# RetNet attention and SwiGLU FFN on one core: the first stage written as one list of steps, with other places for loads, jobs 8 to 11, norms and rounding

## The chip, the cores and the metric

The kernel runs on one core of a Trainium2 chip. The metric is the time of the program on the device in microseconds (us). The engines of a core are named as in the profile: PE (TensorE), DVE (VectorE), ACT (ScalarE), POOL (GpSimd) and SP (SyncE, which issues most DMAs here). Each engine works through its own instructions in program order, and SP's DMAs are issued in the order in which they stand in its queue.

## The reference

```python
# attention: batch 8, heads 8, seq 576, head_dim 64
scores = scale * np.matmul(q, k.transpose(0, 1, 3, 2))
Dmat = np.where(rel >= 0, gamma[:, None, None] ** rel[None, :, :], 0.0)
ret = scores * Dmat[None, :, :, :]
out = np.matmul(ret, v).astype(np.float32)
# FFN on its result: 4608 tokens, d_model 512, d_ff 1536
rms = np.sqrt(np.mean(x * x, axis=-1, keepdims=True) + 1e-06)
xn = x / rms * rms_g
g = xn @ w_gate
silu = g * (1.0 / (1.0 + np.exp(-g)))
val = xn @ w_val
return (silu * val @ w_out).astype(np.float32)
```

The decay `gamma` differs by head; the attention's result, seen as 4608 tokens of 512, is the input of the RMS norm and the FFN. Everything is float32.

## The kernel before

The attention is cut into 32 jobs, a pair of heads of one batch each; four jobs fill one unit of tokens `u` (512 tokens; there are nine). For a job, `load_first`/`load_tails` (jobs 0 to 7) or `fetch` (from job 8 on) load q, k, v; `turn` (jobs 0 to 7, on PE with ACT copying out) or `prepare` (from job 8 on, DVE's transposes, L256) bring q and k into the transposed layout; `scale_v` multiplies v by decay factors on ACT (L265); `slot(j)` issues the matmuls: the values of the job before (L354, L374), and its own scores (L284) and states (L304). `close(j)` issues the values of a job without a slot following. `fetch` issues 13 DMAs on SP: four for q and four for k (L159), two each for k and v (L200), one for v's tail (L203). They wait, if at all, for the buffers of an earlier job.

The FFN of units 2 to 8 uses a block scheme with fewer products (`up`, L594, and `across`, L735), which needs the weights rounded and combined beforehand. That happens in the first stage, `start()`. The weights come in 36 halves (`load_half`, through SP, L858). For each half DVE and ACT extract exponents (`exponent`), mantissas (`mantissa`, L891 and L895), and `join` (L912) puts them together. `weights(n)` goes on by n of these steps, and `weights_to(n)` until n halves are joined. Every fourth half completes a set: POOL combines its blocks (`combine_blocks`, L923), and SP stores them (L948): the `up` sets to `w_up_blocks`, the three `out` slices to `w_out_blocks`, seven stores each. `store_blocks` issues such stores, and `refill` loads pieces of `w_out_blocks` back into the ring of buffers (L564). `act(n)` does n waiting pieces of the jobs' ACT and DVE work (masks, sums, results).

Units 0 and 1 are computed in this stage with `up_plain`: 48 products (`up`, L655) of four 128x128x512 matmuls each, k even for gate (ACT's Silu) and odd for value (a DVE multiply). Then `across(0)` and `across(1)` multiply by w_out, after which `up(2)` begins, which reads the sums of x that `sums_of_x(2)` (L527) makes.

The norm of unit u: `square` (ACT, L430) per job; `gather` (DVE, L440) adds the squares of the four; `norm_1` sums over partitions by a matmul `ms` (L447) with a column of 1/512, adds epsilon on DVE and takes the power -0.5 on POOL; `diagonals` (DVE, L461) writes four diagonal matrices; `norm_2` spreads them by a matmul `rb` (L513) and scales x (DVE, L515). Units from 2 on take `root_1` and `root_2` in place of the power and the diagonals.

The order is written out by the loops of `start()`, and the engines keep to it. Jobs 8 to 11, for unit 2, are interleaved with the up products by number (`now` counts them):

```python
elif now in (41, 44, 46):
    n = {41: 2, 44: 3, 46: 4}[now]
    prepare(FIRST + n)
    fetch(FIRST + n + 1)
```

After product 40, at `(u, k) == (0, 5)`, stands this, ahead of the fetch of job 11 (`now` 41):

```python
weights_to(len(halves))
store_blocks(len(halves) + 9)
refill(1)
```

PSUM has eight banks, and a new tile takes the one that was released longest ago. Halves from the end of the prologue on keep exponents and mantissas in banks (`in_psum`).

Of the kernel before, what the change touches and what calls it, by code (L numbers as in the profile page):

```python
# [11 lines left out]
U32 = mybir.dt.uint32  # L12
# [29 lines left out]
def kernel(  # L42
# [61 lines left out]
    mhalf = cell("mhalf", -0.5)  # L104
    most = cell("most", 1151.0)
# [113 lines left out]
    def turn(j, wait=0):  # L219
# [26 lines left out]
        warm_up(wait, 2 * P)  # L246
# [185 lines left out]

    def gather(u, c, sq):

        if c == NHP - 1 and u > 1:
            nc.vector.scalar_tensor_tensor(
                out=sq, in0=t_of[u], scalar=EPS * DM / P, in1=sq, op0=ALU.add, op1=ALU.add
            )
        elif c:
            nc.vector.tensor_tensor(out=sq, in0=t_of[u], in1=sq, op=ALU.add)  # L440
        t_of[u] = sq

    def norm_1(u):

        ms = bank(f"ms_{u}")
        for s in range(NS):
            nc.tensor.matmul(  # L447
                ms[:, s : s + 1], lhsT=t_of[u][:, s * P : s * P + P], rhs=mean_w,
                start=True, stop=True,
            )  # L450
        r = tmp.tile([P, NS], F32, tag="r", name=f"r_{u}", bufs=1)
        nc.vector.tensor_scalar(out=r, in0=ms[:, :NS], scalar1=EPS, scalar2=None, op0=ALU.add)
        nc.gpsimd.tensor_tensor(out=r, in0=r, in1=mhalf.to_broadcast([P, NS]), op=ALU.pow)
        t_of[u] = r

    def diagonals(u):
# [3 lines left out]
        for s in range(NS):  # L460
            nc.vector.tensor_scalar(  # L461
                out=t_of[u][:, s * P : s * P + P], in0=ident, scalar1=r[:, s : s + 1],
                scalar2=None, op0=ALU.mult,
            )
# [179 lines left out]
    def up_plain(u, k):  # L644


# [3 lines left out]
        for half in range(2):  # L650
            for i in range(2):
                ps = bank(f"up_{u}_{k}_{half}_{i}")
                for c in range(NHP):
                    blk = (A21, A22)[c // 2] if half else (A11, A12)[c // 2]
                    nc.tensor.matmul(  # L655
                        ps, lhsT=w[:, PLACE[blk], c % 2, i * P : i * P + P],
                        rhs=x_of[u][:, c], start=(c == 0), stop=(c == NHP - 1),
                    )
                o = hh[:, half * NH + f + i]
                if m:  # L660
                    nc.vector.tensor_tensor(out=o, in0=o, in1=ps, op=ALU.mult)
                else:
                    nc.scalar.activation(out=o, in_=ps, func=AF.Silu)
                yield
# [166 lines left out]
    for kind, at in (  # L831
        ("up", 0), ("up", 1), ("out", 0), ("up", 2), ("up", 3), ("out", 1), ("up", 4), ("up", 5),
# [35 lines left out]
    def exponent(i):  # L868

        exps[i] = bank(f"exp_{i}") if in_psum else flat_t[i % 2][:, WORDS:]  # L870
# [11 lines left out]
    def mantissa(i):  # L882
# [7 lines left out]
        m = bank(f"man_{i}").bitcast(U32) if in_psum else hi  # L890
# [58 lines left out]

    stores = []  # L950
    in_psum = False
# [45 lines left out]
    READY = (4, 8, 16, 20, 28, 32)  # L997
# [3 lines left out]
    def start():  # L1001

        nonlocal in_psum
# [13 lines left out]
        for j in range(FIRST):  # L1017
            load_first(j)
            if j == 0:
                load_tails(0, range(2))  # L1020
                table(3, nc.sync)
            elif j == 1:
                load_tails(0, range(2, H))
                load_half(0, nc.sync)
            elif j in (2, 4, 5, 7):
                load_half({2: 1, 4: 2, 5: 3, 7: 4}[j], nc.sync)
            if j == 3:
                nc.sync.dma_start(out=rms_g, in_=moe_rms_g.rearrange("(c p) -> p c", p=P))
                load_tails(1, range(H))
                table(4, nc.sync)  # L1030
        turn(0, 1)
        scale_v(0)
        squares = []
        for j in range(FIRST):
            slot(j, rest=(j > 0))
            if j + 1 < FIRST:
                turn(j + 1)
            if squares:
                gather(*squares.pop())
            for i in ((1,), (2,), (3,), (4, 5), (6,), (7,), (), ())[j]:  # L1040
                scale_v(i)
            if j:
                squares.append((*divmod(j - 1, NHP), square(*divmod(j - 1, NHP))))
            act(1)
            if j == 5:
                norm_1(0)
            elif j == 6:
                norm_2(0)
            weights((0, 0, 1, 2, 2, 2, 1, 2)[j])
            if j == 4:  # L1050
                gather(*squares.pop())
            elif j == 5:
# [135 lines left out]
```

## Time and profile before

| | us |
|---|---|
| time, median of 3 runs | 1150.01 |
| the runs | 1149.01 to 1151.32 |
| the profiled run | 1155.01 |
| its span | 1153.2 |
| first up product of `up_plain` starts | 63.60 |
| first product of `across(0)` starts | 271.65 |
| first product of `up(2)` starts | 342.02 |

The profiled execution has a span of its own, so positions and waits are read from it, and differences are carried over to the median. In the profile's rows "x8" counts records, "out<-in" gives the tiles, and brackets hold the idle time of the engine ahead of the first of them and what ended it. Each matmul of float32 by 512 columns leaves two records. PEclk is the clock that was granted to PE, 1.00 being full.

### The profile page before, as it was taken

The page shows a single profiled execution, that of the slowest core. Times are in us where ns is not written, and L with a number is a line of the kernel's source. Part 1 is how long each engine was busy: PE and PEld are TensorE (multiplying, and loading weights), DVE is VectorE, ACT ScalarE, POOL GpSimd, SP SyncE. Part 2 cuts the span into 40 slices and gives each one's busy share as a digit, 9 for nine tenths or more (in the row PEclk, how much of TensorE's full clock was granted, in tenths as well). Part 3 has the DMA queues.
Part 4 walks back from the last instruction along what each step waited for, and adds up shares of the span by engine and source line. Part 5 has one row for each costly group of instructions (what it writes and reads, how often), then busy time and mean ns, then how long its engine had stood idle before and what let it go on. Part 6 is the DMA issues. An engine that isn't in the chain of part 4 may idle for free. (4 is left out here: it accounts for less than half of the span.)

```text
span 1153.2 us, 24145 instructions
## 1 busy us (share of the span) xinstructions
PE 1104.5 (96%) x10086; PEld 918.6 (80%) x10086; DVE 823.4 (71%) x1426; ACT 247.5 (21%) x501; POOL 399.2 (35%) x328
## 2 busy tenths in 40 slices
PE   7789999959999999999999999999999999999997
PEld 6644444437998889888988898889988998898897
DVE  3788979948696778577947795779576944593465
ACT  3633434301102130123012301221122111201110
POOL 0021625443752018301730164006500660173035
PEclk8989999979999999999999999999999999999999
DMA  8644688678987886587768874897576566475461
GB/s 197 173 96 180 235 298 269 197 229 239 325 300 234 229 254 240 168 214 210 268 209 216 239 276 173 203 246 268 192 184 227 191 224 208 147 278 172 160 239 38
DMA packets 255421, 249.22 MB, mean 216 GB/s; under 512 B 193104, under 2 KB 213840, under 8 KB 249168
## 3 DMA queue, kind: packets, MB, share of 16 engines
q1 hardware_dynamic: 253728, 247.11, 68.8%
q8 instruction: 79, 1.29, 0.5%
q10 hardware_dynamic: 1584, 0.56, 0.2%
q14 instruction: 30, 0.25, 0.1%
HBM read 217.55 MB, written 30.08 MB: 215 GB/s over the span
## 5 line engine op out<-in xcount | busy, mean ns | idle before, releaser
L706 POOL TENSOR_TENSOR vi<-h 128x384 f32<-128x384 f32 x64 | 79.5, 1259 | 503.5 <-DVE h L613 453.3
L655 PE MATMUL up<-x,ring 128*128 128x512 f32 x384 | 172.1, 608 | 1.6 <-DVE x L515 0.9
L594 PE MATMUL x<-x,ring 128*128 128x256 f32 x672 | 161.5, 383 | 0.8 <-issue 0.8
L594 PE MATMUL w<-sums,ring 128*128 128x256 f32 x672 | 159.3, 380 | 0.0
L594 PE MATMUL z<-x,ring 128*128 128x256 f32 x672 | 158.7, 379 | 0.0
L655 PEld LDWEIGHTS up<-x,ring 128*128 128x128 f32 x384 | 73.9, 195 | 94.5 <-issue 87.8
L594 PEld LDWEIGHTS z<-x,ring 128*128 128x128 f32 x672 | 127.7, 190 | 19.9 <-issue 2.9
L594 PEld LDWEIGHTS w<-sums,ring 128*128 128x128 f32 x672 | 127.3, 190 | 17.4
L594 PEld LDWEIGHTS x<-x,ring 128*128 128x128 f32 x672 | 125.1, 190 | 18.4 <-issue 1.0
L594 PE MATMUL y<-sums,ring 128*128 128x256 f32 x336 | 79.4, 379 | 0.0
L601 DVE TENSOR_TENSOR h<-u,w 128x512 f32<-128x512 f32 x42 | 28.9, 688 | 65.6 <-PE w L594 65.6
L807 POOL TENSOR_TENSOR vi<-vi 128x512 f32<-128x512 f32 (+1 forms) x56 | 67.2, 1213 | 22.2 <-DVE vi L753 19.7
L594 PEld LDWEIGHTS y<-sums,ring 128*128 128x128 f32 x336 | 63.8, 190 | 8.7
L601 DVE TENSOR_TENSOR u<-m,y 128x512 f32<-128x512 f32 x42 | 28.8, 686 | 50.2 <-PE y L594 50.2
L620 ACT COPY m<-x 128x512 f32<-128x512 f32 x42 | 24.6, 586 | 181.4 <-PE x L594 181.4
L333 DVE SCALAR_TENSOR_TENSOR sum<-sum,gc,s 128x64 f32<-128x64 f32 x192 | 53.9, 281 | 6.8
L615 ACT ACTIVATE h<-h 128x512 f32<-128x512 f32 x63 | 39.7, 630 | 85.0 <-DVE h L601 85.0
L749 ACT COPY vi<-xo 128x512 f32<-128x512 f32 x18 | 10.6, 586 | 207.4 <-PE xo L735 177.7
L923 POOL TENSOR_TENSOR vi<-vi 128x512 f32<-128x512 f32 (+1 forms) x24 | 40.4, 1684 | 36.1 <-DVE vi L912 11.4
L317 DVE SCALAR_TENSOR_TENSOR ret<-s,causal 128x320 f32<-128x320 f32 x64 | 28.8, 485 | 29.6 <-PE s L284 22.2
L923 POOL TENSOR_TENSOR ring<-ring 128x512 f32<-128x512 f32 x24 | 30.5, 1276 | 51.1 <-DMA w_up_blocks<-ring 31.9
L601 DVE TENSOR_TENSOR u<-u,z 128x512 f32<-128x512 f32 x42 | 28.9, 687 | 26.7 <-PE z L594 25.7
(248 smaller groups left out, 2015.4 us busy)
## 6 DMA issues: line engine op xcount, KB each, us to landing
ring<-w_out_blocks SPq DMA_DIRECT2D x63, 1344.0 KB, 6.7
ring<-w_up_blocks SPq DMA_DIRECT2D x42, 1792.0 KB, 8.1
w_out_blocks<-vi SPq DMA_DIRECT2D x21, 448.0 KB, 5.9
out_dram<-vi SPq DMA_DIRECT2D x64, 128.0 KB, 2.6
qraw<-in_q_dram SPq DMA_DIRECT2D x96, 72.0 KB, 5.5
kraw<-in_k_dram SPq DMA_DIRECT2D x96, 72.0 KB, 3.0
k<-in_k_dram SPq DMA_DIRECT2D x48, 128.0 KB, 2.8
v<-in_v_dram SPq DMA_DIRECT2D x48, 128.0 KB, 2.8
```

The source lines that it names most:

```text
L317: nc.vector.scalar_tensor_tensor(out=ret[:, e], in0=s[e][:, : n * L].rearrange("p (c k) -> p c k", k=L), scalar=float(_gamma(H)[2 * hp + e ...
L333: nc.vector.scalar_tensor_tensor(out=t[:, c], in0=t[:, c - 1], scalar=gc[:, hp : hp + 1], in1=part, op0=ALU.mult, op1=ALU.add,)
L594: nc.tensor.matmul(ps[:, i * HU : i * HU + HU], lhsT=w[:, PLACE[blk], c, i * P : i * P + P], rhs=t_of[u][blk][:, c], start=(start and i == ...
L601: nc.vector.tensor_tensor(out=o, in0=a, in1=pairs_of(ps), op=ALU.add)
L615: nc.scalar.activation(out=o, in_=c, func=AF.Silu)
L620: nc.scalar.copy(out=s1, in_=pairs_of(x_))
L655: nc.tensor.matmul(ps, lhsT=w[:, PLACE[blk], c % 2, i * P : i * P + P], rhs=x_of[u][:, c], start=(c == 0), stop=(c == NHP - 1),)
L706: eng.tensor_tensor(out=o, in0=a, in1=b, op=op)
L749: nc.scalar.copy(out=o, in_=ps)
L807: eng.tensor_tensor(out=t[:, :, o], in0=t[:, :, x], in1=t[:, :, y], op=ALU.add)
L923: nc.gpsimd.tensor_tensor(out=t[o], in0=t[x], in1=t[y], op=op)
```

## The change

The loops of `start()` go. A list of loads (`LOADS`) and a string of steps (`PLAN`) take their place. A step is a letter and a number: T turn, V scale_v, S slot, C close, P prepare, F fetch, Q square, G gather, N norm_1, D diagonals, X norm_2, w weights, W weights_to, a act, U a product of `up_plain` (unit, k, n), z store_blocks, r refill, d differences, i inner_sums, A a product of `across`, R root_1, Y root_2, M sums_of_x, k the scaled norm weights, o store. For units 0 and 1 the last of the four squares is no longer added by DVE: `ms` is accumulated over two tiles by twice as many matmuls. Epsilon is added by ACT's Relu with a bias, and the diagonals are ACT's Copy with a scale. The order of the halves has up 4 ahead of out 1.

```diff
+    eps = cell("eps", EPS)
...
-    def turn(j, wait=0):
+    def turn(j):
...
-        warm_up(wait, 2 * P)
+        warm_up(j == 0, 2 * P)
...
+        elif u < 2 and c == NHP - 1:
+            sq = (t_of[u], sq)
...
         ms = bank(f"ms_{u}")
         for s in range(NS):
-            nc.tensor.matmul(
-                ms[:, s : s + 1], lhsT=t_of[u][:, s * P : s * P + P], rhs=mean_w,
-                start=True, stop=True,
-            )
+            for i, sq in enumerate(t_of[u]):
+                nc.tensor.matmul(
+                    ms[:, s : s + 1], lhsT=sq[:, s * P : s * P + P], rhs=mean_w,
+                    start=(i == 0), stop=(i == 1),
+                )
         r = tmp.tile([P, NS], F32, tag="r", name=f"r_{u}", bufs=1)
-        nc.vector.tensor_scalar(out=r, in0=ms[:, :NS], scalar1=EPS, scalar2=None, op0=ALU.add)
+        nc.scalar.activation(out=r, in_=ms[:, :NS], func=AF.Relu, bias=eps)
         nc.gpsimd.tensor_tensor(out=r, in0=r, in1=mhalf.to_broadcast([P, NS]), op=ALU.pow)
...
-            nc.vector.tensor_scalar(
-                out=t_of[u][:, s * P : s * P + P], in0=ident, scalar1=r[:, s : s + 1],
-                scalar2=None, op0=ALU.mult,
+            nc.scalar.activation(
+                out=t_of[u][:, s * P : s * P + P], in_=ident, func=AF.Copy, scale=r[:, s : s + 1]
...
-    def up_plain(u, k):
-
-
+    def up_plain(u, k, n):
+
+        half, i = divmod(n, 2)
+        weights_to(READY[k] - (0 if half else 2))
...
+        sets_used[k] += n == 3
...
-        ("up", 0), ("up", 1), ("out", 0), ("up", 2), ("up", 3), ("out", 1), ("up", 4), ("up", 5),
+        ("up", 0), ("up", 1), ("out", 0), ("up", 2), ("up", 3), ("up", 4), ("out", 1), ("up", 5),
...
-        exps[i] = bank(f"exp_{i}") if in_psum else flat_t[i % 2][:, WORDS:]
+        exps[i] = bank(f"exp_{i}") if i in IN_PSUM else flat_t[i % 2][:, WORDS:]
...
+    IN_PSUM = range(4, 36)
+    PLAN = """
+        a1 a1 T0 V0 S0 T1 V1 S1 V2 T2 a1 S2 V3 Q0 a1 T3 a1 Q1 G0 w1 a1 S3 a1 V4 G1 T4 Q2 w1 a1
+        a1 w1 V5 S4 G2 T5 V6 w1 S5 a1 a1 Q3 G3 w1 T6 S6 F8 Q4 N0 D0 Q5 w1 X0 G4 V7 w1 T7 a1 a1
+        G5 S7 Q6 U000 w1 w1 G6 w1 w1 C7 a1 a1 Q7 a1 G7 a1 a1 a1 a1 a1 w1 U001 N1 a1 a1 w1 U002
+        D1 a1 w1 U003 a1 w1 X1 U100 w1 w1 w1 w1 a1 U101 w1 a1 w1 a1 U010 w1 U102 w1 a1 a1 w1 a1
+        U103 a1 w1 w1 w1 w1 w1 a1 U011 a1 w1 w1 a1 w1 a1 U012 a1 w1 a1 a1 w1 U013 w1 w1 a1 a1
+        U110 w1 w1 w1 w1 a1 w1 U111 w1 a1 a1 w1 w1 U112 a1 w1 a1 a1 U113 U020 a1 a1 w1 a1 a1 w1
+        w1 a1 w1 U021 a1 a1 w1 w1 a1 w1 U022 a1 w1 w1 w1 w1 U120 a1 a1 w1 U121 w1 w1 w1 w1 a1 a1
+        U122 a1 U023 w1 a1 a1 a1 U123 w1 w1 P8 a1 w1 w1 a1 w1 a1 U030 w1 U031 F9 w1 w1 w1 w1 w1
+        w1 U130 a1 U032 w1 a1 w1 w1 a1 U033 P9 w1 a1 a1 w1 w1 a1 a1 U131 a1 w1 a1 U132 a1 w1
+        U133 a1 w1 w1 w1 w1 U040 w1 U041 F10 w1 w1 w1 a1 U042 a1 a1 a1 a1 U043 w1 w1 w1 w1 a1 a1
+        a1 a1 w1 w1 U050 a1 a1 w1 a1 a1 w1 U051 w1 a1 a1 a1 w1 a1 w1 w1 w1 U052 a1 U053 w1 w1
+        W36 a1 U140 a1 S8 P10 a1 U141 a1 F11 S9 U142 z0 U143 a1 a1 r1 a1 a1 d0 a1 a1 d1 U150 a1
+        S10 a1 P11 a1 U151 d2 U152 r2 U153 i0 a1 A0 d5 a1 d4 F12 S11 i1 A0 A0 r99 C11 A0 a1 A0
+        Q8 d3 A0 Q9 A0 A0 G8 Q10 G9 G10 a1 A0 A0 Q11 A0 P12 A0 A0 A0 A0 k0 F13 A0 A1 G11 A1 o0
+        A1 A1 A1 A1 A1 A1 A1 A1 R2 A1 Y2 A1 X2 A1 A1 A1 M2 A1
+    """
+    TAILS = ((0, range(2)), (0, range(2, H)), (1, range(2)), (1, range(2, H)))
+    LOADS = [("table", 3), ("tails", 0), ("job", 0), ("tails", 1), ("job", 1), ("job", 2), ("half", 0), ("tails", 2), ("job", 3), ("half", 1), ("job", 4), ("tails", 3), ("job", 5), ("half", 2), ("job", 6), ("job", 7), ("half", 3), ("half", 4), ("table", 4), ("rms_g", 0)]
...
-    READY = (4, 8, 16, 20, 28, 32)
+    READY = [halves.index(("up", k, 1, 1)) + 1 for k in range(2 * NG)]
...
-        for j in range(FIRST):
-            load_first(j)
-            if j == 0:
-                load_tails(0, range(2))
-                table(3, nc.sync)
-            elif j == 1:
-                load_tails(0, range(2, H))
-                load_half(0, nc.sync)
-            elif j in (2, 4, 5, 7):
-                load_half({2: 1, 4: 2, 5: 3, 7: 4}[j], nc.sync)
-            if j == 3:
-                nc.sync.dma_start(out=rms_g, in_=moe_rms_g.rearrange("(c p) -> p c", p=P))
-                load_tails(1, range(H))
-                table(4, nc.sync)
-        turn(0, 1)
-        scale_v(0)
-        squares = []
-        for j in range(FIRST):
-            slot(j, rest=(j > 0))
-            if j + 1 < FIRST:
-                turn(j + 1)
-            if squares:
-                gather(*squares.pop())
-            for i in ((1,), (2,), (3,), (4, 5), (6,), (7,), (), ())[j]:
-                scale_v(i)
-            if j:
-                squares.append((*divmod(j - 1, NHP), square(*divmod(j - 1, NHP))))
-            act(1)
-            if j == 5:
-                norm_1(0)
-            elif j == 6:
-                norm_2(0)
-            weights((0, 0, 1, 2, 2, 2, 1, 2)[j])
-            if j == 4:
-                gather(*squares.pop())
-            elif j == 5:
-                diagonals(0)
-            act(1)
-        gather(*squares.pop())
-        fetch(FIRST)
-        in_psum = True
-        now = 0
-        for u, k in (
-            (0, 0), (1, 0), (0, 1), (1, 1), (0, 2), (1, 2), (0, 3), (1, 3), (0, 4), (0, 5), (1, 4),
-            (1, 5),
-        ):
-            weights_to(READY[k] - 2)
-            for i, _ in enumerate(up_plain(u, k)):
-                if now == 0:
-                    close(FIRST - 1)
-                    gather(1, NHP - 1, square(1, NHP - 1))
-                elif now == 1:
-                    norm_1(1)
-                elif now == 2:
-                    diagonals(1)
-                elif now == 3:
-                    norm_2(1)
-                elif now == 28:
-                    prepare(FIRST)
-                    fetch(FIRST + 1)
-                elif now == 36:
-                    prepare(FIRST + 1)
-                    fetch(FIRST + 2)
-                elif now == 34:
-                    slot(FIRST, rest=False)
-                elif now in (40, 42, 45):
-                    slot(FIRST + {40: 1, 42: 2, 45: 3}[now])
-                elif now in (41, 44, 46):
-                    n = {41: 2, 44: 3, 46: 4}[now]
-                    prepare(FIRST + n)
-                    fetch(FIRST + n + 1)
-                elif now == 47:
-                    close(FIRST + NHP - 1)
-                weights((3 - now % 2) if now > 3 else 1)
-                act(2)
-                if i == 1:
-                    weights_to(READY[k])
-                now += 1
-            sets_used[k] += 1
-            if (u, k) == (0, 5):
-                weights_to(len(halves))
-                store_blocks(len(halves) + 9)
-                refill(1)
-            elif (u, k) == (1, 4):
-                refill(2)
-                for f in range(0, NH, 2):
-                    differences(0, f)
-                inner_sums(0, 0)
-                inner_sums(0, 1)
-        refill()
-        for f in range(0, NH, 2):
-            differences(1, f)
-        nc.vector.tensor_scalar(
-            out=rms_k, in0=rms_g, scalar1=3.0 / 8.0 * K1, scalar2=None, op0=ALU.mult
-        )
-        for i, _ in enumerate(across(0)):
-            if i in (2, 4, 6, 8):
-                gather(2, i // 2 - 1, square(2, i // 2 - 1))
-        for i, _ in enumerate(across(1)):
-            if i == 0:
-                store(0)
-            elif i == 1:
-                root_1(2)
-            elif i == 4:
-                root_2(2)
-            elif i == 8:
-                norm_2(2)
-                sums_of_x(2)
+        squares, outs = [], [across(0), across(1)]
...
+        tasks = {
+            "S": lambda j: slot(j, rest=j not in (0, FIRST)), "C": close, "T": turn, "V": scale_v,
+            "P": prepare, "F": fetch, "Q": lambda j: squares.append(squared(*divmod(j, NHP))),
+            "G": lambda j: gather(*squares.pop(0)), "N": norm_1, "D": diagonals, "X": norm_2,
+            "w": weights, "a": act, "d": lambda f: differences(f // 3, 2 * (f % 3)),
+            "i": lambda n: inner_sums(0, n), "z": lambda n: store_blocks(len(halves) + 9),
+            "r": refill, "W": weights_to, "A": lambda u: next(outs[u], None), "R": root_1,
+            "Y": root_2, "M": sums_of_x, "o": store,
+            "k": lambda _: nc.vector.tensor_scalar(
+                out=rms_k, in0=rms_g, scalar1=3.0 / 8.0 * K1, scalar2=None, op0=ALU.mult
+            ), "U": lambda n: up_plain(n // 100, n // 10 % 10, n % 10),
+        }
+        for what, i in LOADS:
+            loads[what](i)
+        for step in PLAN.split():
+            tasks[step[0]](int(step[1:]))
```

More of the change, by code (lines that the diff above doesn't have):

```diff
@@ L431, in square, with squared @@
         return t
+    def squared(u, c):
+        return u, c, square(u, c)
     def gather(u, c, sq):
@@ L649, in up_plain @@
         w = set_of(k)
[L650 to L657, printed above, removed]
-                    )
[L659 to L664, printed above, removed]
+        ps = bank(f"up_{u}_{k}_{half}_{i}")
+        for c in range(NHP):
+            blk = (A21, A22)[c // 2] if half else (A11, A12)[c // 2]
+            nc.tensor.matmul(
+                ps, lhsT=w[:, PLACE[blk], c % 2, i * P : i * P + P],
+                rhs=x_of[u][:, c], start=(c == 0), stop=(c == NHP - 1),
+            )
+        o = hh[:, half * NH + f + i]
+        if m:
+            nc.vector.tensor_tensor(out=o, in0=o, in1=ps, op=ALU.mult)
+        else:
+            nc.scalar.activation(out=o, in_=ps, func=AF.Silu)
+        sets_used[k] += n == 3
     def t1_of(u):
@@ L889, in mantissa @@
         )
-        m = bank(f"man_{i}").bitcast(U32) if in_psum else hi
+        m = bank(f"man_{i}").bitcast(U32) if i in IN_PSUM else hi
         nc.vector.tensor_scalar(
@@ L948, in store_blocks @@
                 nc.sync.dma_start(out=o, in_=t)
+    IN_PSUM = range(4, 36)
[18 more added lines that the diff above has]
+    LOADS = [("table", 3), ("tails", 0), ("job", 0), ("tails", 1), ("job", 1), ("job", 2), ("half", 0), ("tails", 2), ("job", 3), ("half", 1), ("job", 4), ("tails", 3), ("job", 5), ("half", 2), ("job", 6), ("job", 7), ("half", 3), ("half", 4), ("table", 4), ("rms_g", 0)]
     stores = []
-    in_psum = False
     n_joined = 0
@@ L995, in weights_to @@
         due = False
-    READY = (4, 8, 16, 20, 28, 32)
+    READY = [halves.index(("up", k, 1, 1)) + 1 for k in range(2 * NG)]
     def start():
-        nonlocal in_psum
         tables = list(zip((causal, gv, gc, gq, gx), (_causal_table(), *_decay_tables(H, D))))
@@ L1106, in start @@
-        refill()
-        for f in range(0, NH, 2):
-            differences(1, f)
-        nc.vector.tensor_scalar(
-            out=rms_k, in0=rms_g, scalar1=3.0 / 8.0 * K1, scalar2=None, op0=ALU.mult
-        )
-        for i, _ in enumerate(across(0)):
-            if i in (2, 4, 6, 8):
-                gather(2, i // 2 - 1, square(2, i // 2 - 1))
-        for i, _ in enumerate(across(1)):
-            if i == 0:
-                store(0)
-            elif i == 1:
-                root_1(2)
-            elif i == 4:
-                root_2(2)
-            elif i == 8:
-                norm_2(2)
-                sums_of_x(2)
+        squares, outs = [], [across(0), across(1)]
@@ new lines, in start @@
+        loads = {
+            "job": load_first, "table": lambda i: table(i, nc.sync),
+            "half": lambda i: load_half(i, nc.sync),
+            "tails": lambda i: load_tails(*TAILS[i]),
+            "rms_g": lambda i: nc.sync.dma_start(
+                out=rms_g, in_=moe_rms_g.rearrange("(c p) -> p c", p=P)
+            ),
+        }
[10 more added lines that the diff above has]
+            ), "U": lambda n: up_plain(n // 100, n // 10 % 10, n % 10),
+        }
```

## The prediction

> **What bounds the kernel now.** I read the page first, then the first 342 us by stage, then what TensorE (PE) waited for there, then the order of time on PE and on SP's queue around the longest wait.
>
> ```profile
> PE 1104.5 (96%) x10086; PEld 918.6 (80%) x10086; DVE 823.4 (71%) x1426; ACT 247.5 (21%) x501; POOL 399.2 (35%) x328
> ```
>
> PE is busy 96% of the span and nothing else is above 71%. So the time is PE's work plus PE's holes, and the change can gain only where PE has holes. Every edit lies ahead of `up(2)`, whose first matmul (L594) starts at 342.02. From there on, all instructions are the same. The next view gives the stages, bounded by the first up product (63.60), the first product of `up_plain(1, 0)` (88.81), the last up products (229.00), the first across product (271.65) and `up(2)` (342). Its columns after the length are busy times.
>
> ```profile
> 0.00:63.60 63.60, 49.22 (x1253) 41.78 (x1253) 36.17 (x118) 30.02 (x78) 2.90 (x14) 0.89 0.73 176
> 63.60:88.81 25.21, 21.36 (x112) 9.65 (x111) 18.83 (x41) 7.33 (x12) 6.57 (x6) 0.86 0.43 88
> 88.81:229.00 140.19, 137.68 (x522) 62.63 (x523) 125.99 (x225) 53.80 (x91) 59.07 (x41) 1.00 0.71 243
> 229.00:271.65 42.65, 29.04 (x393) 15.90 (x391) 19.81 (x47) 4.53 (x13) 14.56 (x12) 0.80 0.77 202
> 271.65:342.00 70.35, 67.12 (x596) 66.29 (x591) 60.25 (x73) 8.02 (x15) 46.44 (x39) 1.00 0.87 305
> ```
>
> PE's holes are 14.4 us, 3.9, 2.5, 13.6 and 3.2. Stages two and four also ran at a mean clock of 0.86 and 0.80. What ended the holes, and the largest of them:
>
> ```profile
> PE s L284 <- DVE kT L256: 11.2, 1, 11.2
> ...
> PE ms L447 <- DVE sq L440: 2.1, 1, 2.1
> ```
> ```profile
> 255.17 1.35 PE L284 MATMUL s<-qT,kT 64*64 64x64 f32 x40 [11.22 <-DVE kT L256]
> 257.03 0.47 PE L304 MATMUL s<-v,k 64*64 64x64 f32 x2 [0.52 <-ACT v L265]
> 258.77 1.00 PE L304 MATMUL s<-v,k 64*64 64x64 f32 x25 [1.27 <-ACT v L265]
> ```
> ```profile
> 235.99 6.00 SPq L948 DMA_DIRECT2D w_out_blocks<-vi  x7
> 242.10 1.10 SPq L564 DMA_DIRECT2D ring<-w_out_blocks  x1
> 243.24 4.53 SPq L159 DMA_DIRECT2D qraw<-in_q_dram  x4
> 247.88 4.40 SPq L159 DMA_DIRECT2D kraw<-in_k_dram  x4
> ```
>
> DVE's transpose is named, but it had itself waited 11.33 us for job 11's q. SP issued that q at 243.24, behind the seven stores of the last w_out slice. Those wait for POOL's combinations (SP waits 19.7 us once at L948; POOL's last run, L923, goes from 223.34 for 12.62 us). So the hole is a place in SP's queue: job 11 behind work that it doesn't need. Afterwards PEclk is 0.50 until about 264.5. That costs some 3.7 us: two up products take 9.01 from 260.68, where two take 7.1 at full clock, and the slot's matmuls before them take some 1.8 more.
>
> **The skill.** "TensorE: Matmul & The Clock Gate" (Part 1: The HAM clock gate) says that about 3.4 us of idleness halve the clock and about 3.4 us of activity restore it, on a free-running window. The trace agrees for the 11.22 us hole, but 2.08 us at 73 us were already followed by slow matmuls, while 1.70 and 1.53 us late in the stage were not. I count any idle of 2 us or more as a risk to the clock. "DMA: Bandwidth & Descriptors" (Anatomy of one DMA) says that a semaphore wait is served by the issuing sequencer before dispatch; the 19.7 us that hold job 11 agree.
>
> **The change, part by part.** Durations are from the profiled execution (span 1153.2, run time 1155.01; the other runs 1149.01 to 1151.32). I sum differences against its span and take them off 1150.0.
>
> *To the first up product: +2.5 (-0.5 to +7).* SP now issues the gq table and tails of jobs 0 to 1 ahead of job 0: four DMAs at 0.6 to 0.65 on SP, so `turn(0)` starts 2 to 2.5 later. Then tails and jobs come earlier than halves, so 1.2, 1.4 and 0.4 of PE's waits for q, k and their tails go; by `turn(1)` it is even, within 1. `scale_v` ahead of `turn` on ACT, and other places for gathers and squares, save about 1.0 + 1.1 (s L304 on ACT, av L374 on POOL's tick). A new wait comes at N0 D0 X0: they stand together between slot 6 and turn 7, with nothing of PE between the ms and the rb matmuls. The chain is ACT's Relu 0.3, POOL's pow 1.39, four ACT diagonals, and hops. A diagonal isn't in the trace. The nearest rows are 337 ns (64x64) and 499 ns (128x256) with a scale; "ScalarE: Activation LUTs" (What ACT_TABLE_LOAD costs) prices 280 ns + 0.833 per element for a pointer operand, overlapping by 93, thus 0.29 in a row (an estimate). I take 1.3 for four, ends 1.2 and 2.0. That makes 3.2 to 3.6 idle, and turn 7 and slot 7 are queued behind. With 0.5 for the doubled ms matmuls (four take 1.02), and 1 for the clock: +5, less 2.1 saved and 0.4 of tail waits: +2.5. If ACT's place hides the chain it is nothing; with a long slow clock +7.
>
> *First up product to `up_plain(1, 0)`: -6.3 (-3 to -7.5).* C7, Q7, G7 now follow the second product with rounding between them, so PE has no ms matmul waiting on the last square: 2.08 goes, with 0.57 (ring L912) and 0.28 (tick). With them goes the slow clock after 75 (a product is eight records of 0.44; four took 3.08 instead of 1.76, twelve 7.33 instead of 5.28: 3.3 together). Doubled ms +0.5. X1's 0.9 stays. The old 25.2 becomes 18.9.
>
> *To the last up products: nothing (-1 to +4).* PE's work stays, 3.5 per product. DVE sheds the diagonals (0.87 + 2.90), r (2 x 0.15) and two gather adds (2 x 0.7), some 5.5. ACT takes on 3.2 (eight diagonals, two Relus), with 53.8 busy in that stage. Both are hidden, because DVE sets nothing there: the third stage has 125.99 us of its work in 140.19, which leaves it 14. The order up4 before out1 leaves four halves between the last two out slices where eight lay, so the next slice's first join comes closer to the stores (landing in 5.9) that free `vi`: a wait of about 1 on DVE, 0 to 3 on PE.
>
> *Slots 8 to 11 and the last products: -18 (-10 to -20).* F11, 13 DMAs, stands before S9 and before z0 (the w_out stores), so it leaves SP about 24 us before slot 11 needs it, at 8 to 12 for its issue. So 11.22 + 0.52 + 1.27 and the 3.7 of clock go, and 1.2 + 1.1 (s L284, last L304 on L895), with whose roundings the slots no longer share a place. C11, 1.3 of PE, moves out of this stage into across. That is -20.3. I add back 0.5 for that join and 1.5 to 2 for slots that now stand closer together, each on a transpose and a tick of its own (0.5 to 0.6 at tick L363 before). What F11 jumps is delayed by its 8 to 12 us on SP at most; the stores wait for POOL anyway, whose L923 run would end about 19 us after the 40th product. With 6 for the seven stores, 5.9 for their landing and 6.7 for the refill's, the first w_out piece is there at about +34 to +36, and across starts at +38 (eight products and four slots).
>
> *Across: +1.5 (-1 to +6).* PE's work is 65. C11 adds 1.3; the 1.70 wait for w_out stays (0 to 3: the third piece is now behind F12's 13 DMAs), the 1.53 for POOL too. At the end R2, Y2, X2 and M2 stand after the 10th, 11th, 12th and last-but-one products, where they were after 1, 4 and 8. DVE's queue behind product 13 is: adds 3.5, inner sums 4.4, root 3 to 5, X2 2.73, adds 2.4, then M2's 2.1, some 20 us. PE has about 16 of products left, so `up(2)`, which reads M2's sums, waits about 4 (1 to 6). 65 + 1.3 + 1.5 + 4 = 71.8 against 70.35.
>
> The sum: +2.5 - 6.3 + 0 - 18 + 1.5 = -20.3; I take 20: 1153.2 becomes 1133, and in the runs 1150.0 - 20 = 1130. The eps cell, `sets_used` and READY cost nothing: one memset in the first microseconds while loads run, and no instruction.
>
> **Rivals.** *(a) The wait returns elsewhere (0.25).* The refill-after-store chain has 4 to 6 us of slack; if POOL's combinations end 10 us late, or X0 and M2 both bring a slow clock, 10 of the gain are paid back: about 1140. For: L948's wait was POOL's. Against: POOL is 35% busy. *(b) All goes (0.15).* The earlier jobs hide the N0 chain, and M2 waits under 1: 2.5 + 3.5 + 2 more: 1122. *(c) Rounding becomes the bound, slower (0.07).* Up products take banks least recently released first, and halves 4 to 35 keep exponents and mantissas in banks; the written list puts up to six rounding steps between products. Price: the 1.2 and 1.1 us at L895 are this wait. 20 / 1.2: from 17 of the 48 products so held it is slower than before; with 25, +10: 1160. Against: DVE's 14 us of slack. *(d) The change doesn't do what it says (0.03):* F11 leaves early, but its q buffers come free late; q then lands with slot 11 and the hole stays, 1146 (20 less 16). The old F11 waited for no buffer.
>
> **How the numbers follow.** The likeliest case has 0.50 and 1125 to 1136. (a) reaches to 1143, (b) down to 1120; 1120 to 1143 leaves out (c), (d) and the edges. A difference of 0.2% (2.3 us) is about what a measurement of this kernel can tell from none. Slower by more: (c), 0.07. Within: 0.03 from (a) and (d) at their worst. Faster: 0.90.
>
> **What would show it.** Right: no wait at L284 above 2 us after 200, PEclk at 1.00 from 90 to 300, job 11's q on SP ahead of the last L948 stores, `up(2)` at 319 to 325. A new PE wait of 3 us at rb (L513 before) on ACT near 60, and of 4 at the first L594 on L527's sums. Wrong: up products with waits for rounding lines in rows, across waiting on w_out_blocks, or `up(2)` later than 335.

## The result and the profile after

The changed kernel takes 1138.55 us (median of 3 runs, 1137.28 to 1139.87) against 1150.01: the ratio is 0.990, interval 0.9875 to 0.9924. That is 11.5 us faster, where 20 were forecast: inside the stated range of 1120 to 1143, but outside the 1125 to 1136 that was called the likeliest. A second set of runs gave 0.9919 (0.9893 to 0.9945).

The stages of the changed kernel, cut at the same events as in the prediction, but with one more cut at the end of the 41st up product (217.62 before, 207.25 now). The columns are the length and the busy times of PE, weight load, DVE, ACT and POOL, then PEclk, the DMA share and GB/s. First the kernel after, then those two stages of the kernel before that the extra cut makes new.

```profile
0.00:60.18 60.18, 47.95 (x1261) 40.08 (x1261) 37.83 (x119) 32.06 (x83) 2.62 (x14) 0.94 0.85 199
60.18:80.02 19.84, 18.72 (x122) 9.76 (x119) 13.03 (x32) 8.17 (x16) 6.08 (x6) 1.00 0.25 74
80.02:207.25 127.23, 127.23 (x297) 56.15 (x297) 112.88 (x187) 50.76 (x85) 53.62 (x37) 1.00 0.81 267
207.25:240.31 33.06, 32.87 (x549) 18.22 (x548) 29.30 (x66) 5.52 (x15) 20.50 (x14) 1.00 0.66 209
240.31:318.98 78.67, 71.50 (x665) 69.39 (x659) 60.06 (x87) 9.25 (x20) 46.46 (x41) 0.98 0.92 295
318.98:1137.90 818.92, 802.90 (x7224) 724.19 (x7222) 567.38 (x928) 143.90 (x292) 270.93 (x217) 0.99 0.67 210
```
```profile
88.81:217.62 128.81, 128.67 (x368) 57.18 (x368) 115.11 (x197) 50.03 (x82) 53.32 (x37) 1.00 0.75 255
217.62:271.65 54.03, 38.05 (x546) 21.35 (x545) 30.69 (x75) 8.30 (x22) 20.31 (x16) 0.84 0.66 181
```

The stage with the hole shrinks from 54.03 to 33.06, and PE is busy for 32.87 of that, at full clock. The stage ahead of it is all PE's work before and after. But the across products take 78.67 where they took 70.37, and the rest of the kernel, whose instructions are the same, 818.92 where it took 811.18. So 16 us were given back. The longest waits of PE in the changed kernel, those of its first 45 us left out, are these; the one at rb lies in the first stage, the others in across or right behind it:

```profile
PE y L600 <- DVE sums L533: 4.4, 1, 4.4
PE wo L740 <- DMA ring<-w_out_blocks: 2.8, 1, 2.8
PE rb L519 <- ACT diag L468: 2.8, 1, 2.8
...
PE wp L740 <- POOL vi L711: 1.9, 2, 1.5
PE xp L740 <- issue: 1.6, 1, 1.6
```

(L600 is L594 of the kernel before, L533 is L527, L740 is L735, L519 is L513.) SP's queue has become what the step said: job 11 (215.74) is ahead of the seven stores. Job 11's first load had itself stood 13.5 us in the queue for a buffer, until DVE had transposed job 10's q (first line of the second fence), but it came early enough; and the stores behind it waited only 0.9 for POOL, where they had waited 19.7.

```profile
215.74 2.10 SPq L160 DMA_DIRECT2D qraw<-in_q_dram  x4
...
224.18 6.29 SPq L953 DMA_DIRECT2D w_out_blocks<-vi  x7
230.56 2.00 SPq L570 DMA_DIRECT2D ring<-w_out_blocks  x2
232.78 8.24 SPq L160 DMA_DIRECT2D qraw<-in_q_dram  x4
...
248.92 22.41 SPq L570 DMA_DIRECT2D ring<-w_out_blocks  x7
```
```profile
SPq L160 <- DVE qT L257: 13.7, 2, 13.5
...
SPq L953 <- POOL vi L928: 0.9, 1, 0.9
```

The end of the first stage on DVE, in order of time (L758 adds products, L483 to L502 are the root, L521 is X2, L533 is M2), and POOL beside it:

```profile
303.76 0.69 DVE L758 TENSOR_TENSOR vi<-vi,yo 128x512 f32<-128x512 f32 x1 [5.33 <-DMA ring<-w_out_blocks]
...
310.44 0.68 DVE L483 SCALAR_TENSOR_TENSOR e<-e,ms 128x512 f32<-128x512 f32 x1
...
314.81 2.74 DVE L521 SCALAR_TENSOR_TENSOR x<-x,rms_k,sq 128x512 f32<-128x512 f32 x4
...
319.78 0.55 DVE L758 TENSOR_TENSOR vi<-vi,wp 128x384 f32<-128x384 f32 x1
320.25 1.57 DVE L533 TENSOR_TENSOR sums<-x 128x512 f32<-128x512 f32 x1
321.85 1.63 DVE L533 TENSOR_TENSOR x<-x 128x512 f32<-128x512 f32 x1
323.52 1.63 DVE L533 TENSOR_TENSOR sums<-x 128x512 f32<-128x512 f32 x1
```
```profile
320.00 10.51 POOL L812 TENSOR_TENSOR vi<-vi 128x512 f32<-128x512 f32 x7 [7.21 <-DVE vi L758]
```

M2 stands behind the adds of the last across product (319.78), so it can't start before PE is through with that product (318.98): the step of the plan that follows M2 brings no product, only POOL's last combination (L812). Each of M2's subtractions takes 1.6 beside that combination. In the kernel before, the same subtractions took 0.69 each and were over before POOL began (first fence below). The changed kernel has its third sum at 325.15. Behind the wait the clock is slow, 0.50 from 324 to 330; the second fence has ten microseconds around it, with the columns of the stages.

```profile
339.07 0.69 DVE L527 TENSOR_TENSOR sums<-x 128x512 f32<-128x512 f32 x1
...
343.73 5.32 POOL L807 TENSOR_TENSOR vi<-vi 128x512 f32<-128x512 f32 x4 [8.35 <-DVE vi L753]
```
```profile
322.00:332.00 10.00, 6.70 (x20) 5.54 (x21) 6.01 (x5) 0.00 (x0) 8.27 (x6) 0.66 0.76 321
```

### The profile page after: what moved, and what is told of

Read it like the earlier page. It is cut to its first block, busy times and chain, and to the rows that moved or that the text cites. A ratio compares the mean times of both kernels' runs of the same rounds, so it can differ in the third digit from the quotient of the medians.

```text
span 1137.9 us, 24174 instructions
## 1 busy us (share of the span) xinstructions
PE 1101.2 (97%) x10102; PEld 917.8 (81%) x10102; DVE 820.5 (72%) x1415; ACT 249.7 (22%) x511; POOL 400.2 (35%) x328
## 5 line engine op out<-in xcount | busy, mean ns | idle before, releaser
L711 POOL TENSOR_TENSOR vi<-h 128x384 f32<-128x384 f32 x64 | 78.2, 1237 | 496.3 <-DVE h L619 460.6
L660 PE MATMUL up<-x,ring 128*128 128x512 f32 x384 | 166.6, 594 | 0.8 <-DVE x L521 0.8
L600 PE MATMUL x<-x,ring 128*128 128x256 f32 x672 | 161.4, 383 | 0.0
L600 PE MATMUL z<-x,ring 128*128 128x256 f32 x672 | 159.4, 380 | 0.0
L600 PE MATMUL w<-sums,ring 128*128 128x256 f32 x672 | 159.3, 380 | 0.0
L600 PEld LDWEIGHTS z<-x,ring 128*128 128x128 f32 x672 | 128.3, 191 | 20.2 <-issue 2.9
L600 PEld LDWEIGHTS w<-sums,ring 128*128 128x128 f32 x672 | 127.3, 190 | 17.4
L600 PEld LDWEIGHTS x<-x,ring 128*128 128x128 f32 x672 | 125.1, 190 | 17.4
L600 PE MATMUL y<-sums,ring 128*128 128x256 f32 x336 | 81.2, 385 | 4.4 <-DVE sums L533 4.4
L812 POOL TENSOR_TENSOR vi<-vi 128x512 f32<-128x512 f32 (+1 forms) x56 | 69.0, 1244 | 21.1 <-DVE vi L758 18.6
L607 DVE TENSOR_TENSOR h<-u,w 128x512 f32<-128x512 f32 x42 | 28.9, 687 | 65.7 <-PE w L600 48.8
L600 PEld LDWEIGHTS y<-sums,ring 128*128 128x128 f32 x336 | 64.8, 193 | 13.8 <-issue 4.8
L607 DVE TENSOR_TENSOR u<-m,y 128x512 f32<-128x512 f32 x42 | 28.8, 685 | 50.4 <-PE y L600 50.4
L607 DVE TENSOR_TENSOR u<-u,z 128x512 f32<-128x512 f32 x42 | 28.8, 687 | 26.9 <-PE z L600 25.9
L711 POOL TENSOR_TENSOR vi<-h,vi 128x384 f32<-128x384 f32 x32 | 45.3, 1416 | 2.5
```

The costliest lines, as they stand in the source:

```text
L600: nc.tensor.matmul(ps[:, i * HU : i * HU + HU], lhsT=w[:, PLACE[blk], c, i * P : i * P + P], rhs=t_of[u][blk][:, c], start=(start and i == ...
L607: nc.vector.tensor_tensor(out=o, in0=a, in1=pairs_of(ps), op=ALU.add)
L660: nc.tensor.matmul(ps, lhsT=w[:, PLACE[blk], c % 2, i * P : i * P + P], rhs=x_of[u][:, c], start=(c == 0), stop=(c == NHP - 1),)
L711: eng.tensor_tensor(out=o, in0=a, in1=b, op=op)
L812: eng.tensor_tensor(out=t[:, :, o], in0=t[:, :, x], in1=t[:, :, y], op=ALU.add)
```

## The experiments

The first table gives the ratio to the kernel before, run on the same chip in the same series. There were three series (e1 to e4; a0 and e5 to e7; e8 to e10 and b0), in which the kernel before took 1152.57, 1151.43 and 1150.79 us. So kernels of different series are compared here by their ratios, not by their medians. The second gives the stages of each profile: to the first up product, from there to `up_plain(1, 0)`, to the first across product, to `up(2)`, and the rest.

| kernel | median us | ratio, interval |
|---|---|---|
| e1_f11_late | 1148.64 | 0.9972, 0.9960 to 0.9985 |
| e2_before_f11_early | 1145.47 | 0.9942, 0.9920 to 0.9965 |
| e5_before_p12_late | 1140.13 | 0.9903, 0.9882 to 0.9924 |
| a0_after_again | 1143.10 | 0.9919, 0.9893 to 0.9945 |
| e3_m2_early | 1135.26 | 0.9853, 0.9829 to 0.9877 |
| e4_x0_after_t7 | 1138.75 | 0.9890, 0.9866 to 0.9915 |
| e6_m2_mid | 1136.27 | 0.9866, 0.9843 to 0.9889 |
| e7_combined | 1136.21 | 0.9863, 0.9843 to 0.9884 |
| e8_g11_early_all | 1130.62 | 0.9814, 0.9801 to 0.9826 |
| e9_loads_before | 1143.77 | 0.9944, 0.9930 to 0.9958 |
| e10_norm_before | 1142.05 | 0.9927, 0.9910 to 0.9944 |
| b0_before_again | 1151.47 | 1.0012, 1.0000 to 1.0024 |

| profile | first up | to u=1 | to across | to `up(2)` | rest | span |
|---|---|---|---|---|---|---|
| before | 63.6 | 25.2 | 182.8 | 70.4 | 811.2 | 1153.2 |
| b0_before_again | 62.4 | 23.4 | 182.6 | 70.4 | 811.3 | 1150.1 |
| after | 60.2 | 19.8 | 160.3 | 78.7 | 818.9 | 1137.9 |
| a0_after_again | 62.5 | 19.8 | 160.3 | 78.0 | 819.6 | 1140.2 |
| e1_f11_late | 66.7 | 19.8 | 168.9 | 77.9 | 818.1 | 1151.3 |
| e2_before_f11_early | 60.8 | 25.1 | 177.1 | 70.6 | 811.4 | 1144.9 |
| e5_before_p12_late | 60.9 | 23.5 | 165.4 | 79.9 | 811.3 | 1141.0 |
| e3_m2_early | 60.2 | 19.8 | 160.3 | 81.2 | 812.0 | 1133.5 |
| e4_x0_after_t7 | 56.4 | 19.8 | 160.3 | 77.3 | 819.3 | 1133.2 |
| e6_m2_mid | 60.8 | 19.8 | 160.3 | 81.2 | 812.8 | 1134.9 |
| e7_combined | 57.6 | 20.2 | 160.3 | 81.4 | 812.0 | 1131.5 |
| e8_g11_early_all | 58.2 | 19.8 | 160.3 | 80.3 | 812.2 | 1130.9 |
| e9_loads_before | 68.3 | 19.8 | 160.3 | 77.6 | 820.5 | 1146.5 |
| e10_norm_before | 62.1 | 19.4 | 160.3 | 78.0 | 819.3 | 1139.0 |

Read the second table first for what repeats: 160.3 in nine profiles of the new plan, and a first column that moves by 6 us between kernels whose first 60 us are the same code (after, a0, e1, e3, e6: 60.2 to 66.7). So an effect in that column needs the timed runs; the others can be read from one profile, to about 1 us.

**The kernels themselves again.**

> The changed kernel itself, unaltered, as the base for the kernels beside it and to see how much its own profile differs from one execution to the next. All theories: 0.987 to 0.992 of the kernel before. The first 60 us (waits on loads, with whatever clock follows) may differ by several us; the stages from the first up product on should repeat within 1 us.

> The kernel before itself, for a second profile. The recorded profile had a span of 1153.2 with run times of 1149.0 to 1151.3 beside it. Expected: span 1147 to 1152, the hole at job 11 again 8 to 12 us with a slow clock behind it, and the difference to the first profile in the first 60 us or in the length of the hole, with all stages after up(2) within 1 us.

As expected, except that the hole in b0 was 12.89 (expected 8 to 12), and that part of b0's difference (1.8) lies in the second stage, where it was not looked for. The repeats differ from the first profiles by +2.3 and -3.1, mostly in the first 90 us. This is why the profiles' difference (15.3 in the first pair, 9.9 in the second) surrounds the 11.5 of the runs.

**Job 11's place in SP's queue.**

```diff
-        W36 a1 U140 a1 S8 P10 a1 U141 a1 F11 S9 U142 z0 U143 a1 a1 r1 a1 a1 d0
+        W36 a1 U140 a1 S8 P10 a1 U141 a1 S9 U142 z0 U143 a1 a1 r1 F11 a1 a1 d0
```

> The changed kernel with one step put back: F11 (job 11's 13 DMAs) stands after z0 and r1 in SP's queue, as before, and nothing else is moved. Theory (the gain is the place of F11 ahead of the w_out stores): the hole at L285 comes back with 8 to 11 us of PE idle and a clock of 0.50 after it, and the time is 12 to 17 us above the changed kernel's 1138.6, so 1151 to 1156, no better than the kernel before. Rival (the gain comes from the up products and the prologue): under 4 us, up to 1142.

The old wait is back, at half its length:

```profile
250.42 1.35 PE L285 MATMUL s<-qT,kT 64*64 64x64 f32 x40 [5.11 <-DVE kT L257]
```

The edit takes back 8.6 us of the stage, wait and slow clock together, and its ratio goes from 0.990 or 0.992 to 0.997. So the place of F11 is worth some 6 to 8 us in the runs, less than the 12 to 17 expected: with the other steps of the plan where they are, the hole is half as long. Why it is shorter there was not tried.

**The same edit, alone, in the kernel before.**

```diff
             if (u, k) == (0, 5):
+                fetch(FIRST + 3)
                 weights_to(len(halves))
...
-                    fetch(FIRST + n + 1)
+                    if n != 2:
+                        fetch(FIRST + n + 1)
```

> The kernel before with one step of the change: job 11's fetch is issued ahead of the w_out stores, after product 40. Theory: the 11.2 us hole goes with its slow clock, 1150.0 becomes 1133 to 1138, about as good as or better than the whole change, since this kernel keeps its early sums of x. Rival: the DMAs jumped ahead only move the wait to the first across product (w_out pieces), and it stays within 4 us of 1150.

The hole at job 11 is gone, and this stands in its place on PE (first fence), because of this on ACT (second):

```profile
261.88 1.13 PE L374 MATMUL av<-qT,sum 64*64 64x64 f32 x32 [10.01 <-ACT tick L363]
```
```profile
259.97 0.51 ACT L265 ACTIVATE v<-v,gv 128x256 f32<-128x256 f32 x1 [17.16 <-DMA v<-in_v_dram]
...
261.65 0.17 ACT L363 COPY tick<-mhalf 1x1 f32<-1x1 f32 x1
```

ACT had reached `prepare` of job 12, whose v was now the load behind the w_out stores. It stood there for 17.16, and the tick that close(11) waits for (a copy of one element on ACT, for which PE waits) was next in ACT's order. The time is 0.994, between the two forecasts. Moving one load moved the wait to the next one, on another engine. A second edit takes job 12 out of that stage:

```diff
-                elif now in (41, 44, 46):
-                    n = {41: 2, 44: 3, 46: 4}[now]
+                elif now in (41, 44):
+                    n = {41: 2, 44: 3}[now]
...
             if i in (2, 4, 6, 8):
                 gather(2, i // 2 - 1, square(2, i // 2 - 1))
+            elif i == 10:
+                prepare(FIRST + 4)
+            elif i == 13:
+                fetch(FIRST + 5)
```

> The kernel before with job 11's fetch ahead of the w_out stores and, in addition, prepare of job 12 and fetch of job 13 moved from product 47 into across(0). Theory: with the fetch alone, ACT's scale of job 12's v (a load behind those stores) held the tick that close(11) waits for, 10.0 us; with both moved neither wait is there, and up(2) starts 10 to 14 us earlier than with the fetch alone: 0.981 to 0.987 of the kernel before, where the fetch alone gave 0.994. Rival: a third wait takes their place (w_out pieces at the first across products), and it stays at 0.992 to 0.996.

The stage falls to 165.4, near the plan's 160.3. Of the 5.1 between them, 2.7 are waits that the plan doesn't have (1.23 and 1.11 of slots for roundings, 0.34 for a tick), and 1.5 is close(11), which the plan has in across. But across grows from 70.6 to 79.9, so `up(2)` starts only 3.8 earlier than with the fetch alone, where 10 to 14 were expected: as the rival had said, w_out pieces now come late (4.23, 0.55 and 1.51 of waiting, with a slow clock after the first two). The first of them:

```profile
263.69 2.90 PE L735 MATMUL wo<-ring,h 128*128 128x128 f32 x12 [4.23 <-DMA ring<-w_out_blocks]
```

At 0.990 these two edits of the old loops give as much as the whole change, within the intervals. Across lengthens as in the changed kernel: in both, the refill of the third w_out piece stands behind job 12's loads in SP's queue, and PE now comes to it earlier.

**Where the sums of x stand.** Three tries, of which the last also has the two edits of the next part:

```diff
-        k0 F13 A0 A1 G11 A1 o0 A1 A1 A1 A1 A1 A1 A1 A1 R2 A1 Y2 A1 X2 A1 A1 A1 M2 A1
+ e3     k0 F13 A0 A1 G11 o0 A1 R2 A1 A1 A1 Y2 A1 A1 A1 A1 X2 M2 A1 A1 A1 A1 A1 A1 A1
+ e6     k0 F13 A0 A1 G11 A1 o0 A1 A1 A1 R2 A1 A1 Y2 A1 A1 X2 M2 A1 A1 A1 A1 A1 A1 A1
+ e8     P12 A0 G11 A0 A0 A0 k0 F13 A0 A1 A1 o0 R2 A1 A1 A1 Y2 A1 A1 A1 A1 X2 M2 A1 A1 A1 A1 A1 A1 A1
```

> The changed kernel with R2, Y2, X2 and M2 at about the steps of across(1) where the kernel before has them (after the 2nd, 5th and 9th). Theory: the 4.4 us wait of the second product of up(2) on L533's sums goes, and the slow clock of 322 to 331 with it, 7 us in all: 1131 to 1133, and the four subtractions of L533 take 0.7 each in place of 1.6, because POOL then doesn't run its last combination beside them. Rival (DVE's queue is full in across(1), so the wait moves into the across products): 1136 to 1140.

> The changed kernel with R2 after the 5th, Y2 after the 7th, X2 and M2 after the 9th step of across(1). Theory: root_1's matmul no longer waits for the last gather (6.5 us when it stood after the 2nd step), M2 ends before POOL starts its combination and before the last across product, so neither wait is there: 0.979 to 0.983 of the kernel before, 8 to 11 us under the changed kernel. Rival: DVE's queue is the limit and one of the across products or y waits 3 us or more: 0.985 to 0.990.

In both, the wait of y is gone, L533 takes 0.69 per subtraction, and the rest falls from 818.9 to 812.0 and 812.8: the 4.43 and the slow clock behind it were worth 6 to 7 us. But both got a new wait in across, again with a slow clock, one line of each:

```profile
287.19 2.05 PE L477 MATMUL ms<-sq,ones 128*128 128x512 f32 x2 [6.48 <-DVE sq L440]
```
```profile
302.49 1.65 PE L740 MATMUL yp<-ring 128*128 128x128 f32 x6 [5.37 <-DVE e L490]
```

In e3 the root's matmul waits for the last gather (G11), which stands behind the combination at the end of across(0) in DVE's order. In e6 the gather is done, but the matmul's bank is read by DVE's root until L490, and product y, the first to need that bank, waits for it. Net gain against the two sets of the changed kernel (0.990 and 0.9919): 0.005 to 0.007 of the time (e3) and 0.003 to 0.005 (e6). Neither got what was hoped for, and e6 lies in its rival's range.

**The norm's chain, and the third w_out piece.**

```diff
-        N0 D0 Q5 w1 X0 G4 V7 w1 T7 a1 a1
+        N0 D0 Q5 w1 G4 V7 w1 T7 X0 a1 a1
...
-        d4 F12 S11
+        d4 r3 F12 S11
```

> The changed kernel with X0 moved behind T7, so that turn 7 (about 3.3 us of matmuls) lies between the ms and the rb matmuls. Theory: the 2.8 us wait at rb goes and with it the slow clock of 50 to 58 (about 3 us): 4 to 6 us less, 1133 to 1135. Rival (the next up products wait for x, so the time only moves to the first up product): 1137 to 1139.

The first edit alone. The wait at rb is gone, and the first up product starts at 56.4; e7 and e8, which share the edit, have 57.6 and 58.2, all below the 60.2 to 66.7 of the five profiles named above. The runs, 1135.1 to 1143.9, do not tell it from the changed kernel. So: visible in the profiles, inconclusive in the time.

> The changed kernel with three edits: the places of R2, Y2, X2, M2 as in the run beside it, X0 behind T7, and the third w_out piece ahead of F12 in SP's queue (r3 F12). Theory (each wait is on PE's path and they add up): 0.974 to 0.979 of the kernel before, about 1124 to 1130. Rival (the earlier end of one runs into the next): no better than the M2 edit alone by more than 0.002.

Both edits and e6's places: 0.9863, no better than e6 alone, as the rival said. The third w_out piece was no longer waited for, but product y then waited 1.31 for its inner sums (DVE, L711), and the yp wait stayed at 5.44.

> The changed kernel with X0 behind T7 and r3 ahead of F12, and with G11 moved from across(1) to the steps behind P12, so that R2 can stand after the 2nd step of across(1), Y2 after the 5th, X2 and M2 after the 9th, as in the kernel before. Theory (R2 needs G11 early, and its bank free before product y): no wait over 2 us at ms, yp, or the first y of up(2), no slow clock after 280, up(2) at 308 to 314: 0.973 to 0.979 of the kernel before. Rival (DVE has no room in across(1) for the root, whatever its place): a wait of 3 us or more shows elsewhere in across(1), and it is 0.984 to 0.988, like the two kernels with X2 and M2 in the middle.

This is the best kernel: 0.9814, against 0.9863 for e7, from which it differs by the places of G11 and the root alone; the intervals don't meet. No wait stands at ms, yp or y. It stayed short of the expected 0.973 to 0.979, though better than its rival, because across still takes 80.3 and not the 70 to 76 that an `up(2)` at 308 to 314 needed: w_out pieces are waited for twice (1.86 and 2.82), and both times the clock drops to 0.50.

```profile
257.94 1.92 PE L740 MATMUL yo<-ring,h 128*128 128x128 f32 x12 [1.86 <-DMA ring<-w_out_blocks]
294.44 0.94 PE L740 MATMUL wo<-ring,vi 128*128 128x128 f32 x6 [1.53 <-POOL vi L711]
302.89 2.44 PE L740 MATMUL xo<-ring 128*128 128x128 f32 x12 [2.82 <-DMA ring<-w_out_blocks]
```

**Loads and norm.** In e9 `LOADS` has the order of the kernel before; in e10 the norm has DVE's add, epsilon and diagonals and four ms matmuls again, at the plan's places:

```diff
-    LOADS = [("table", 3), ("tails", 0), ("job", 0), ("tails", 1), ("job", 1), ("job", 2), ("half", 0), ...
+    LOADS = [("job", 0), ("tails", 0), ("table", 3), ("job", 1), ("tails", 1), ("half", 0), ("job", 2), ...
```

> The changed kernel with the loads in the order of the kernel before (job 0 first, its tails and the gq table behind it, halves earlier). My step said that the new order costs 2 to 2.5 us at the first turn and gives as much back by job 1. Theory (loads are a wash): within 0.3% of the changed kernel, 0.988 to 0.995 of the kernel before. Rival (the new order is worth several us of the first 60): 0.995 or more, with waits of 1 us and more on DMA at turn_q and turn_t.

> The changed kernel with the norm's edits undone and the steps left where they are: DVE adds the fourth square, four ms matmuls in place of eight, DVE adds epsilon and writes the diagonals. Theory (the engines' shares are worth nothing, the places are): PE sheds 1 us, DVE takes on 5.5 that lie beside the up products, the wait at rb stays 2.5 to 4: within 0.2% of the changed kernel, 0.990 to 0.994. Rival (DVE's queue delays the chain): rb waits 5 us or more and the stage to the first up product grows, 0.994 to 0.998.

e9 ended at 0.9944, inside the theory's range but at its edge, and with a wait that the rival had named: on DMA at the turn of job 1's tails (1.83, then 0.33). It is 0.25% above the second set of the changed kernel, with intervals that overlap (0.9930 to 0.9945), and 0.44% above the first, with intervals that don't. So the new order of loads is more likely worth something than nothing, 3 to 5 us if so. e10 is at 0.9927, not told from 0.9919: which engine adds the squares and writes the diagonals makes no difference that can be measured. The wait at rb is 3.96 by DVE instead of 2.77 by ACT, and the stage after it is 0.4 shorter by the halved ms matmuls.

## Why the prediction was right where it was, and where not

*The hole: right, and undersized.* `-18` for slots 8 to 11, with nothing for the products before: measured 182.84 to 160.29, -22.5. The products up to the 41st are unchanged (127.23, and 128.81 with slot 8 before). What I added back (0.5 for a join, 1.5 to 2 for "slots closer together") did not come: the stage has 0.2 us of PE idle. Over both stages PE's idle fell by 15.9, where the waits counted make 15.3, and its busy time by 6.6 (166.72 to 160.10), where 3.7 of slow clock and 1.3 of C11 were counted. e1 and e2 show F11's place to be a cause, and e2 shows what the step left out: taken alone, the wait goes to the load behind it. P12 has to move as well, as e5 shows; the prediction has no term for that move. Its terms for the first w_out piece (19, 6, 5.9 and 6.7) add to 37.6 and not to 34 to 36, but no product waited for that piece.

*First up product to `up_plain(1, 0)`: right.* -6.3 forecast (its own terms make -5.7, since the 0.5 for the doubled ms was not added), -5.4 against the first profile, and -3.6 against the repeat, where the same wait (2.18) was followed by no slow clock (1.00 from 72 to 84).

*To the first up product: the parts right, the sum not shown.* The new wait is there: forecast 3.2 to 3.6, measured 2.77, with ACT's Relu 0.26 and four diagonals 1.28 (1.3 taken). The clock fell during it and was 0.50 from 52 to 56. But +2.5 isn't seen: 60.2 to 66.7 now and 60.8 to 63.6 before can't be told apart. e9 suggests that the loads give back 3 to 5 us, where I had them even, but does not settle it.

*Across and the sums of x: the step that was wrong in size.* The term was `65 + 1.3 + 1.5 + 4 = 71.8 against 70.35`, thus +1.5. That sum was wrong before any run: PE's work there was 67.12 in the prediction's own table, not 65, and the 1.70 wait that "stays" was left out. 67.12 + 1.70 + 1.53 are the 70.35, so the new terms, 1.3 and 4, made +5.3. Measured: +8.3 to `up(2)` and +7.7 behind it, 16.0. The wait of `up(2)` was forecast at 4 and came at 4.43, but by luck, since two errors cancel. The DVE queue was reckoned at 20 us with M2 2.1; M2's third sum came 21.4 after 303.76 because the subtractions took 1.6 each. And the first product needs no sum, only the second does. M2 was also said to stand after the last-but-one product; it stands after the last. The slow clock behind it (0.50 from 324 to 330), named as a rival's part and left out of the sum, cost most of the remaining 3.3: PE is busy 2.9 longer with the same instructions (802.90 against 800.05). In across itself PE's busy time grew from 67.14 to 71.50, 1.5 of it close(11), about as much a slow clock at 296 to 300 (in the repeat, without it, PE is busy 69.92), and the idle from 3.2 to 7.2: 2.78 for the third piece behind F12 (within the 0 to 3 given; 1.70 before), 1.65 at xp that the profile names "issue", 0.44 at the tick and 0.64 for POOL and a w_out piece.

*The total: in the range, partly by luck.* Across and what is behind it were missed by 14.5 us; the slots came out 4.5 better than forecast, and the first stage 5.9 better, where profiles of the same code differ by as much.

*The rivals.* What happened is nearest to (a), "The wait returns elsewhere", whose 1140 is closer to the measured 1138.55 than the 1130 forecast: X0 and M2 both brought a slow clock. Its other reason, late combinations on POOL, did not come. Of the -23.0 by which `up(2)` starts earlier (342.02 to 318.98), 7.7 are lost right behind. (c) did not happen: from 80.02, 37 up products run without an idle gap. (d) came true in half: job 11's load did wait for its buffer (13.5 us), which the prediction had not counted on, but the hole did not stay.

*Left open.* The order of the halves, the banks for exponents and mantissas and the new places of the rounding steps were not tried on their own. Why xp waits 0.5 to 1.7 for "issue" after the first four groups of across in most profiles of the plan was not tried, nor was an order of SP's refills that frees both w_out pieces.

## What to carry to other kernels

A load that waits behind a store in one issue queue holds everything behind it, so moving one load forward moves the wait to the next; follow the queue until the last load that is needed early, and look at which engine stops for it (here ACT, with another job's tick behind). When a sum at the end of a stage is put late, ask what it stands behind on its engine, and who runs beside it at that time. Short PE waits of 2 to 5 us may bring a slow clock, and the price then grows: 2.9 us of PE time behind the 4.43. They don't always: behind the 2.78 at 256.60 PEclk stayed at 1.00.

## What was not expected of the hardware

- A DVE subtraction of 128x512 with two inputs in SBUF took 0.69 alone and 1.6 while POOL ran L812 beside it. POOL's seven took 10.51, and 9.11 in e3 and e6, where M2 was over before. A DVE add with one input in PSUM (L607 at 329.16 in the changed kernel) took 0.69 beside the same combination. The Trainium skill ("GPSIMD Engine Reference", 1. Specifications) says that POOL's SBUF interface is shared with VectorE and contends with instructions of two SBUF inputs; the trace agrees, and gives the price here: 2.3 times for DVE.
- In e7 the clock fell to 0.50 at 52 to 54 with PE hardly idle (below), behind sixteen records of 128x1 matmuls (1.95 us) and job 7's turn. In e4 and e8, with the same order, PEclk stayed at 1.00, and so it did behind the other sixteen 128x1 records of the changed kernel (69.50). What lowered it in e7 is open.

```profile
48.00:50.00 2.00, 2.00 (x19) 1.99 (x20) 1.72 (x8) 0.05 (x1) 0.00 (x0) 1.00 0.97 273
50.00:52.00 2.00, 2.00 (x20) 1.52 (x18) 1.93 (x7) 0.86 (x4) 1.02 (x1) 0.80 1.33 219
52.00:54.00 2.00, 1.95 (x6) 0.79 (x4) 1.31 (x2) 2.00 (x7) 0.00 (x0) 0.50 1.02 110
```
